# Packed attention and a mixture of experts: the values of both halves multiplied in one burst, a gate chain with fewer VectorE operations, and one addition moved to ScalarE

## The chip, the cores and the metric

The kernel runs on one core of one Trainium2 chip. The metric is the device time in microseconds (us), the median of three runs; less is better. A core has TensorE (PE, matmuls; PEld is its weight load), VectorE (DVE), ScalarE (ACT), GpSimd (POOL) and SyncE (SP, which here only issues DMAs). Each engine works through its own instructions in the order in which they were written, and waits for the others by semaphores.

## The reference, cut to what matters

q, k and v are 8 batches x 8 heads x 576 x 64, p (the "packs") is 8 x 8 x 32 x 64. The attention runs twice: the packs attend over the keys, and the queries attend over the 32 packed rows. Its result feeds a mixture of 8 experts.

```python
def sm_attn(qq, kk, vv):
    s = scale * np.matmul(qq, kk.transpose(0, 1, 3, 2))
    s = s - np.max(s, axis=-1, keepdims=True)
    a = np.exp(s)
    a = a / (np.sum(a, axis=-1, keepdims=True) + 1e-09)
    return np.matmul(a, vv)
p_packed = sm_attn(p, k, v)
out = sm_attn(q, p_packed, p_packed)
...
logits = np.einsum('bsd,de->bse', x, w_gate)          # x: out, 8 x 576 x 512
local_gate = 1.0 / (1.0 + np.exp(-np.einsum('bsd,de->bse', x, w_local).squeeze(-1)))
for b in range(B):
    prev_e = -1
    for s in range(S):
        fresh_e = int(np.argmax(logits[b, s]))
        if s == 0 or local_gate[b, s] < 0.5:
            e = fresh_e
        else:
            e = prev_e if prev_e >= 0 else fresh_e
        prev_e = e
        ls = logits[b, s] - logits[b, s].max()
        p = np.exp(ls)
        p /= p.sum() + 1e-09
        h = np.maximum(x[b, s] @ w1[e], 0.0)          # 512 -> 1024
        out[b, s] = p[e] * (h @ w2[e])                # 1024 -> 512
```

## The kernel before, in words

Each of the 8 batches goes through stages, with its 8 heads in two halves (Q = 0 and 1) of four heads. **Packs:** L496 multiplies packs by keys, L514 takes the scores out of PSUM, L551 transposes the weights of a half (three transposes, then two), L553 copies them to SBUF as `a1T`, and L567 multiplies them by the values: 20 matmuls for a half, each on a tile of 32 columns of the array, which the profile counts as 40 instructions; L583 transposes the result into `ppT`. **Queries:** L614, the softmax over 32 packed rows at L630 to L661 (L652 sums, L654 adds 1e-9, L656 inverts), and the split of the result into a high and a low part (`a2h`, `a2l`). **Gates:** L873 and L881 make the logits, L888 transposes them (`lt`), and a chain of small VectorE operations (L896 to L960) finds the expert's number `e` of the batch (from the first token), the softmax weight `pe`, and a flag `stray` for tokens that would go to another expert. A stray anywhere starts a general branch at the program's end; with these inputs it isn't taken. From `e` the SyncE queue starts the loads of the expert's weights (L987, `w1t`; L994, `w2raw`). L1028 folds the first weights with the packed rows. **Expert:** all of it in pairs of high and low parts. The first layer (L1054) makes six matmuls for half the tokens of 128 hidden units; ScalarE (L1065) and VectorE (L1070, the low part) take the result out and so free its PSUM bank. The second layer (L1094, L1099 and L1103) adds into five accumulators `acc0` to `acc4`. GpSimd forms the low part of the second weights (L1083).

Three PSUM banks are passed around for everything but the accumulators. The order of all engines is fixed when the program is built: each stage is a Python generator, and a planner (`weave`, with the costs of a `Clock`) takes a step of one generator after another, the expert of one batch being the main thread and the attention of the next filling in. A `yield need(...)` is where it may switch; it puts no wait of its own into the program. The expert of a batch takes some 50 us, and in that time the attention and gates of the next one run.

Below, L1054 and so on are lines of the kernel before. In the changed kernel the same lines are 9 to 18 further down: L1063 is the first layer, L1103 and L1108, L1112 the second, L1079 the low part on VectorE, L582 the values, L600 the transposes behind them, L906 and L914 the start of the gate chain, L821 the expert's number.

Of the kernel before, what the change touches and what calls it, by code (L numbers as in the profile page):

```python
# [168 lines left out]
def packed_attn_moe_kernel(  # L169
# [355 lines left out]
    def keys(st, Q):  # L525
# [17 lines left out]
        rooms = ("w2s", "w2s") if st["early"] and Q == 1 else ("a1T", "a1U")  # L543
        yield need(s2, slot=(("w2s", 2),) if st["early"] and Q == 1 else rooms)
# [57 lines left out]
    def queries(st, Q):  # L602
# [262 lines left out]
    def gates(st, expert=None):  # L865
# [31 lines left out]
        mxb = mx.unsqueeze(2).broadcast_to([128, NB, E])  # L897
        v0 = tile_([128, 1], F32, "v0")
# [471 lines left out]
```

## Time and profile before

| what | before |
|---|---|
| median of 3 runs | 428.78 us (428.70 to 429.36) |
| profiled execution: its time, its span | 428.42 us, 426.6 us |
| busy share: TensorE, VectorE, ScalarE, GpSimd | 97%, 63%, 44%, 26% |
| chain that ended last: TensorE, VectorE, ScalarE | 85%, 10%, 2% |

The span is the part of an execution between its first and last recorded instruction. The chain that ended last is followed back from the last instruction, at each step to what released it; its shares say on whom the end waited.

### The profile page before, as it was taken

How to read it: one execution, taken by the hardware profiler on the slowest of the kernel's cores; microseconds unless marked ns; L12 is line 12 of the kernel's file. 1: busy time of each engine (PE TensorE's matmuls, PEld its weight loads, DVE VectorE, ACT ScalarE, POOL GpSimd, SP SyncE). 2: the span in 40 equal slices, each digit the busy share in tenths (PEclk: the TensorE clock that was granted, in tenths of full speed). 3: DMA queues.
4: the chain of work that ended last, by engine and by line, in shares of the span. 5: the costliest groups of instructions: out<-in, count | busy, mean ns of one | idle time of the engine just before them, and what ended most of it. 6: DMA issues, size and time to landing. Idle time of an engine off the chain costs nothing.

```text
span 426.6 us, 9843 instructions
## 1 busy us (share of the span) xinstructions
PE 411.9 (97%) x3735; PEld 317.2 (74%) x3736; DVE 269.0 (63%) x771; ACT 187.5 (44%) x438; POOL 111.1 (26%) x123
## 2 busy tenths in 40 slices
PE   8899999999999999999999998999989999999994
PEld 6676766876777787678768885788857888688882
DVE  4597688685976597667933888348772696422122
ACT  2564434553435443564354541645335443443221
POOL 1005022421541224115312161122511136123220
PEclk9999999999999999999999999999999999999998
DMA  8789749974996593959986947489191212721003
GB/s 225 236 305 231 140 96 324 179 224 104 320 174 212 146 191 77 383 153 167 246 291 110 174 147 258 153 157 224 62 346 28 98 40 87 285 98 37 2 1 115
DMA packets 160909, 72.98 MB, mean 171 GB/s; under 512 B 131170, under 2 KB 139610, under 8 KB 160858
## 3 DMA queue, kind: packets, MB, share of 16 engines
q1 hardware_dynamic: 160858, 72.32, 65.0%
q8 instruction: 30, 0.49, 0.5%
q14 instruction: 21, 0.17, 0.1%
HBM read 62.87 MB, written 9.44 MB: 169 GB/s over the span
## 4 chain that ended last, share of the span: by engine, by line
PE 85%; DVE 10%; ACT 2%; DMA 1%; issue 1%; SPq 0%; DVEq 0%; ACTq 0%
PE acc L1094 40%; PE bank L1054 23%; PE bank L1028 4%; PE acc L1099 3%; PE acc L1103 3%; PE bank L567 2%; PE bank L551 2%; PE bank L614 2%; DVE qn L453 2%; DMA raw<-in_k_dram 1%; PE bank L496 1%; DVE h L1070 1%; PE bank L873 1%; DVE vc L901 1%; DVE df L931 1%
## 5 line engine op out<-in xcount | busy, mean ns | idle before, releaser
L1094 PE MATMUL acc<-w2s,h 128*128 128x512 f32 x768 | 209.7, 404 | 0.0
L1094 PEld LDWEIGHTS acc<-w2s,h 128*128 128x128 f32 x768 | 134.7, 188 | 34.3 <-issue 11.9
L1083 POOL TENSOR_TENSOR w2s<-w2raw,w2s 128x512 fp32r<-128x512 f32 x64 | 85.7, 1341 | 263.7 <-ACT w2s L1081 246.4
L1070 DVE SCALAR_TENSOR_TENSOR h<-bank,h 128x64 fp32r<-128x64 f32 (+3 forms) x192 | 61.5, 347 | 81.6 <-ACT h L1065 80.6
L1065 ACT ACTIVATE h<-bank 128x288 fp32r<-128x288 f32 (+2 forms) x128 | 52.8, 412 | 113.2 <-PE bank L1054 106.0
L1054 PEld LDWEIGHTS bank<-a2h,wph 128*128 128x128 f32 x256 | 45.4, 188 | 24.8 <-issue 6.5
L1054 PE MATMUL bank<-a2h,wph 128*128 128x288 f32 (+2 forms) x256 | 57.8, 307 | 4.7 <-DVE gsm L940 2.9
L1054 PE MATMUL bank<-a2l,wph 128*128 128x288 f32 (+2 forms) x256 | 54.9, 296 | 0.0
L1054 PE MATMUL bank<-a2h,wpl 128*128 128x288 f32 (+2 forms) x256 | 54.8, 295 | 0.0
L1054 PEld LDWEIGHTS bank<-a2h,wpl 128*128 128x128 f32 x256 | 41.2, 188 | 0.0
L1054 PEld LDWEIGHTS bank<-a2l,wph 128*128 128x128 f32 x256 | 40.9, 188 | 0.0
L1081 ACT CAST w2s<-w2raw 128x512 fp32r<-128x512 f32 x64 | 39.5, 617 | 0.2
L1038 DVE TENSOR_TENSOR wpl<-bank,wph 128x512 fp32r<-128x512 f32 (+1 forms) x32 | 20.0, 664 | 18.1 <-ACT wph L1035 18.1
L1035 ACT CAST wph<-bank 128x512 fp32r<-128x512 f32 (+1 forms) x32 | 16.8, 576 | 24.1 <-PE bank L1028 24.1
L1099 PE MATMUL acc<-w2s,h 128*128 128x512 f32 x64 | 26.4, 412 | 0.0
L1103 PE MATMUL acc<-w2s,h 128*64 128x512 f32 x64 | 25.3, 395 | 0.0
L669 POOL TENSOR_TENSOR a2l<-a2t,a2h 128x576 fp32r<-128x576 f32 x14 | 20.0, 1439 | 10.7 <-ACT a2h L667 8.2
L1123 ACT ACTIVATE o<-acc,pe 128x512 f32<-128x512 f32 x23 | 15.8, 688 | 11.3 <-PE acc L1094 11.0
L632 DVE STREAM_TRANSPOSE sT<-bank 128x288 f32<-128x288 f32 x28 | 11.8, 460 | 11.4 <-ACT gate L630 10.9
L599 DVE STREAM_TRANSPOSE qn<-qn 128x1152 f32<-128x1152 f32 x14 | 19.0, 1365 | 0.0
L553 ACT COPY a1T<-bank 116x384 f32<-116x384 f32 (+1 forms) x28 | 11.6, 428 | 12.3 <-PE bank L551 11.9
L453 DVE STREAM_TRANSPOSE qn<-qn 128x1152 f32<-128x1152 f32 x12 | 16.3, 1360 | 0.1
(190 smaller groups left out, 427.8 us busy)
## 6 DMA issues: line engine op xcount, KB each, us to landing
w2raw<-in_moe_w_dram SPq DMA_DIRECT2D x64, 256.0 KB, 7.8
w1t<-in_moe_w_dram SPq DMA_DIRECT2D x15, 1024.0 KB, 5.4
kv<-in_v_dram SPq DMA_DIRECT2D x16, 560.0 KB, 9.8
out_dram<-o SPq DMA_DIRECT2D x32, 256.0 KB, 3.4
qn<-in_q_dram SPq DMA_DIRECT2D x28, 288.0 KB, 4.9
qn<-in_k_dram SPq DMA_DIRECT2D x24, 288.0 KB, 5.2
raw<-in_k_dram SPq DMA_DIRECT2D x4, 576.0 KB
raw<-in_q_dram SPq DMA_DIRECT2D x2, 576.0 KB
```

Source lines behind the costliest of these rows:

```text
L453: nc.vector.transpose(out=kT, in_=kT)
L599: nc.vector.transpose(out=qT, in_=qT)
L669: nc.gpsimd.tensor_tensor(out=a2l, in0=a2t, in1=a2h.bitcast(F32), op=ALU.subtract)
L1038: nc.vector.tensor_tensor(out=lo[:, Q, cols], in0=ts[Q][:, :width], in1=hi[:, Q, cols].bitcast(F32), op=ALU.subtract,)
L1054: nc.tensor.matmul(out=t[:, :width], lhsT=st["wp"][c // 4][wi][:, Q, fs], rhs=a2[ai][Q][:, ts], start=(n == 0), stop=(n == 5),)
L1065: nc.scalar.activation(out=h[:, lo:hi], in_=t[:, :hi - lo], func=AF.Relu)
L1070: nc.vector.scalar_tensor_tensor(out=h[:, dst:dst + z - a], in0=t[:, a:z], scalar=0.0, in1=h[:, lo + a:lo + z].bitcast(F32), op0=ALU.max, ...
L1081: nc.scalar.copy(out=w[:, 0], in_=raw)
L1083: rest.tensor_tensor(out=w[:, 1], in0=raw, in1=w[:, 0].bitcast(F32), op=ALU.subtract)
L1094: nc.tensor.matmul(out=acc, lhsT=hs[hi], rhs=w[:, wi], start=(c == 0 and n == 0), stop=(c == NC - 1 and n == 2),)
L1099: nc.tensor.matmul(out=acc, lhsT=h[:, 512:S + TAIL], rhs=w[:, 0], start=(c == 0), stop=False, skip_group_check=True,)
L1103: nc.tensor.matmul(out=acc[0:TAIL], lhsT=h[:, 512:S], rhs=w[:, 1], start=False, stop=(c == NC - 1), skip_group_check=True,)
```

## The change

Three edits, and what the planner makes of them. First, the values: the generator `keys` of each half ended with its own burst L567; now both halves end in one generator, `packed_keys`, which multiplies both (80 instructions) behind one another into one bank, scales both, transposes both and copies them out once. The first batch, which goes by halves, stays as it was. The buffers of the transposed weights become two pairs, those of the packed rows three for both halves instead of six for one. Second, the gate chain: the subtraction of the maximum (`under`) is made once and serves the expert's code `vc` and the exponent; the softmax weight of the chosen expert is taken by its column in a multiplication on GpSimd, where a mask, a product and a reduction stood; the local gate and the stray flags are worked out once for all batches (`strays`). Per batch the chain has 9 VectorE operations where it had 21. Third, the addition of 1e-9 at L654 goes from VectorE to ScalarE (L672).

```diff
-    "kv": 2, "qn": 3, "p_in": 2, "q_in": 1, "zz": 2, "a1": 2, "a1T": 1, "a1U": 1, "ppT": 6, "sT": 2, "a2t": 2,
+    "kv": 2, "qn": 3, "p_in": 2, "q_in": 1, "zz": 2, "a1": 2, "a1T": 2, "a1U": 2, "ppT": 3, "sT": 2, "a2t": 2,
...
-        rooms = ("w2s", "w2s") if st["early"] and Q == 1 else ("a1T", "a1U")
-        yield need(s2, slot=(("w2s", 2),) if st["early"] and Q == 1 else rooms)
+        rooms = ("a1T", "a1U")
+        yield need(s2, slot=rooms)
...
-        yield need(*a1T, st["v", Q], slot="zz", banks=1)
+        st["turned", Q] = a1T, rs
+        if st["early"]:
+            yield from packed_keys(st, (Q,))
+        elif Q == NQ - 1:
+            yield need(when=lambda: ("turned", 0) in st)
+            yield from packed_keys(st, range(NQ))
+
+    def packed_keys(st, Qs):
+
+        if 0 in Qs:
+            st["ppq"] = tile_([128, NQ, 128], F32, "ppT")
+            clock.edges[st["ppq"].tensor.name] = (128,)
+        a1T, rs = zip(*(st["turned", Q] for Q in Qs))
+        yield need(*(x for y in a1T for x in y), *vs, slot="zz", banks=1)
         pp = bank()
-        for c in range(NV):
-            rows = slice(0, VP if c == 0 else VP - 1)
-            for h in range(HQ):
-                nc.tensor.matmul(
-                    out=pp[32 * h:32 * h + 32, :D],
-                    lhsT=a1T[c // J3][rows, c % J3, 32 * h:32 * h + 32],
-                    rhs=st["v", Q][rows, h, D * c:D * c + D],
-                    start=(c == 0), stop=(c == NV - 1),
-                )
-        give(*a1T, st["v", Q])
-        zz = tile_([128, 2, D], F32, "zz")
-        wide = pp[:, :D].unsqueeze(1).broadcast_to([128, 2, D])
-        if st["early"]:
-            nc.vector.tensor_scalar(out=zz, in0=wide, scalar1=rs, scalar2=None, op0=ALU.mult)
+            for c in range(NV):
+                rows = slice(0, VP if c == 0 else VP - 1)
+                for h in range(HQ):
+                    nc.tensor.matmul(
+                        out=pp[32 * h:32 * h + 32, D * n:D * n + D],
+                        lhsT=a1T[n][c // J3][rows, c % J3, 32 * h:32 * h + 32],
+            wide = pp[:, D * n:D * n + D].unsqueeze(1).broadcast_to([128, 2, D])
+            if st["early"]:
+                nc.vector.tensor_scalar(out=zz[:, n], in0=wide, scalar1=rs[n], scalar2=None, op0=ALU.mult)
+            else:
+                nc.scalar.activation(out=zz[:, n], in_=wide, func=AF.Copy, scale=rs[n][:, 0:1])
         give(pp)
         yield need(zz, banks=1)
         tp = bank()
-        nc.tensor.transpose(out=tp[:, :128], in_=zz.rearrange("a r d -> a (r d)"), identity=ident)
+        for n, Q in enumerate(Qs):
+            nc.tensor.transpose(out=tp[:, 128 * n:128 * n + 128], in_=zz[:, n].rearrange("a r d -> a (r d)"), identity=ident)
         give(zz)
-        ppq = tile_([128, 128], F32, "ppT")
-        nc.scalar.copy(out=ppq, in_=tp[:, :128])
+        lo, hi = Qs[0], Qs[-1] + 1
+        nc.scalar.copy(out=st["ppq"][:, lo:hi], in_=tp[:, :128 * len(Qs)].rearrange("a (q x) -> a q x", x=128))
         give(tp)
-        st["ppT"][Q] = ppq
+        for Q in Qs:
+            st["ppT"][Q] = st["ppq"][:, Q]
...
-        nc.vector.tensor_scalar(out=sm, in0=sm, scalar1=1e-9, scalar2=None, op0=ALU.add)
+        nc.scalar.activation(out=sm, in_=sm, func=AF.Copy, bias=1e-9)
...
+        under = tile_([128, NB, E], F32, "under")
+        yield need(mx)
+        nc.vector.tensor_tensor(out=under, in0=lg, in1=mx.unsqueeze(2).broadcast_to([128, NB, E]), op=ALU.subtract)
             vc = tile_([128, NB, E], F32, "vc")
-            nc.vector.tensor_tensor(out=vc, in0=lg, in1=mxb, op=ALU.is_equal)
-            yield need(vc)
-            nc.vector.tensor_tensor(out=vc, in0=vc, in1=code.unsqueeze(1).broadcast_to([128, NB, E]), op=ALU.mult)
+            yield need(under)
+            nc.vector.scalar_tensor_tensor(
+                out=vc, in0=under, scalar=0.0, in1=code.unsqueeze(1).broadcast_to([128, NB, E]), op0=ALU.is_equal, op1=ALU.mult,
+            )
-
-            yield need(codes_all, st["e0"])
-            e0 = nc.gpsimd.value_load(st["e0"][0:1, 0:1], min_val=0, max_val=E - 1)
-            nc.gpsimd.tensor_copy(out=v0, in_=code[:, bass.ds(e0, 1)])
-            nc.gpsimd.tensor_copy(out=v0_all[:, b:b + 1], in_=v0)
-            yield need(v0)
...
-        nc.vector.tensor_tensor(out=ex, in0=lg, in1=mxb, op=ALU.subtract)
-        sel = tile_([128, E], F32, "sel")
-        nc.vector.tensor_scalar(out=sel, in0=code, scalar1=v0, scalar2=None, op0=ALU.is_equal)
-        yield need(ex)
-        nc.scalar.activation(out=ex, in_=ex, func=AF.Exp)
+        yield need(under)
+        nc.scalar.activation(out=ex, in_=under, func=AF.Exp)
-            gz = tile_([128, NB], F32, "gz")
-            nc.scalar.activation(out=gz, in_=lt[:, :, E], func=AF.Exp, scale=-1.0)
-            df = tile_([128, NB], F32, "df")
-            nc.vector.tensor_scalar(out=df, in0=cd, scalar1=v0, scalar2=None, op0=ALU.not_equal)
+            nc.scalar.activation(out=fresh_all[:, b], in_=lt[:, :, E], func=AF.Exp, scale=-1.0)
-        nc.vector.tensor_tensor(out=ex, in0=ex, in1=sel.unsqueeze(1).broadcast_to([128, NB, E]), op=ALU.mult)
-        if expert is None:
-            yield need(gz)
-            nc.vector.tensor_scalar(out=gz, in0=gz, scalar1=1.0, scalar2=None, op0=ALU.add)
-        if expert is None:
-            yield need(gz)
-            nc.vector.reciprocal(out=gz, in_=gz)
-        yield need(ex)
-        nc.vector.reduce_sum(out=pe, in_=ex, axis=AX.X)
         if expert is None:
-            fr = fresh_all[:, b]
-            yield need(gz)
-            nc.vector.tensor_scalar(out=fr, in0=gz, scalar1=0.5, scalar2=None, op0=ALU.is_lt)
-            nc.vector.memset(fr[0:1, 0:1], 1.0)
-        yield need(sm, pe)
-        nc.vector.tensor_tensor(out=pe, in0=pe, in1=sm, op=ALU.mult)
-        if expert is None:
-            yield need(fresh_all, df)
-            nc.vector.tensor_tensor(out=df, in0=df, in1=fr, op=ALU.mult)
-            yield need(df)
-            nc.vector.reduce_max(out=stray[:, b:b + 1], in_=df, axis=AX.X)
+            yield need(codes_all, st["e0"])
+            expert = nc.gpsimd.value_load(st["e0"][0:1, 0:1], min_val=0, max_val=E - 1)
+            nc.gpsimd.tensor_copy(out=v0_all[:, b:b + 1], in_=code[:, bass.ds(expert, 1)])
             st["done"] = True
+        yield need(sm)
+        nc.gpsimd.tensor_tensor(out=pe, in0=ex[:, :, bass.ds(expert, 1)].squeeze(2), in1=sm, op=ALU.mult)
         st["pe"] = pe
...
+    def strays(st):
+
+        yield need(when=lambda: all("done" in x for x in sts))
+        nc.vector.tensor_scalar(out=fresh_all, in0=fresh_all, scalar1=1.0, scalar2=None, op0=ALU.add)
+        nc.vector.reciprocal(out=fresh_all, in_=fresh_all)
+        nc.vector.tensor_scalar(out=fresh_all, in0=fresh_all, scalar1=0.5, scalar2=None, op0=ALU.is_lt)
+        nc.vector.memset(fresh_all[0:1, :, 0:1], 1.0)
+        df = sb.tile([128, B, NB], F32, name="df", bufs=1)
+        yield need(codes_all, v0_all)
+        nc.vector.tensor_tensor(out=df, in0=codes_all, in1=v0_all.unsqueeze(2).broadcast_to([128, B, NB]), op=ALU.not_equal)
+        nc.vector.tensor_tensor(out=df, in0=df, in1=fresh_all, op=ALU.mult)
+        nc.vector.reduce_max(out=stray, in_=df.rearrange("a b n -> a (b n)"), axis=AX.X)
+        st["strays"] = True
...
+                yield need(stray, banks=1, when=lambda: "strays" in sts[B - 1])
-                nc.tensor.matmul(out=tot[0:1, 0:1], lhsT=red, rhs=ones_col, start=True, stop=True)
+                nc.tensor.matmul(out=tot[0:1, 0:1], lhsT=stray, rhs=ones_col, start=True, stop=True)
```

On VectorE the gate stage of one of the middle batches reads so before (`lt` are the logits, L1070 frees the bank of a first-layer product, `qn` and `p_in` are keys and packs of the batch after):

```order
L888 STREAM_TRANSPOSE lt<-bank_3642 128x160
L1070 SCALAR_TENSOR_TENSOR h<-bank_3634,h 128x224
L1070 SCALAR_TENSOR_TENSOR h<-bank_3634,h 128x64
L896 TENSOR_REDUCE gmx<-lt 128x5
L901 TENSOR_TENSOR vc<-lt,gmx 128x40
L903 TENSOR_TENSOR vc<-vc,code 128x40
L906 TENSOR_REDUCE codes_all<-vc 128x5
L803 TENSOR_SCALAR e_3687<-codes_all 1x1
L453 STREAM_TRANSPOSE qn<-qn 128x4x288
L1070 SCALAR_TENSOR_TENSOR h<-bank_3676,h 128x288
L920 TENSOR_TENSOR ex<-lt,gmx 128x40
L922 TENSOR_SCALAR sel<-code,v_3669 128x8
```

and so with the change, from the same transpose of the logits on:

```order
L906 STREAM_TRANSPOSE lt<-bank_3531 128x160
L914 TENSOR_REDUCE gmx<-lt 128x5
L453 STREAM_TRANSPOSE qn<-qn 128x4x288
L917 TENSOR_TENSOR under<-lt,gmx 128x40
L1079 SCALAR_TENSOR_TENSOR h<-bank_3557,h 128x224
L1079 SCALAR_TENSOR_TENSOR h<-bank_3557,h 128x64
L921 SCALAR_TENSOR_TENSOR vc<-under,code 128x40
L926 TENSOR_REDUCE codes_all<-vc 128x5
L821 TENSOR_SCALAR e_3587<-codes_all 1x1
L939 TENSOR_REDUCE gsm<-ex 128x5
L417 STREAM_TRANSPOSE p_in<-p_in 128x256
L453 STREAM_TRANSPOSE qn<-qn 128x4x288
```

One `qn` transpose, `under` and an L1079 now stand ahead of `vc` and of the expert's number `e`; `sel`, `df` and the second product of `vc` are gone, and the second transpose and the L1079 that ends this piece come sooner after `e`.

On TensorE the values of one of these batches read so before (`kv` are the values, `zz` the scaled result):

```order
L567 MATMUL bank_3917<-kv,a1T 32x64 x20
L1094 MATMUL acc_3533<-w2s,h 128x512 x3
L583 MATMUL bank_3949<-ident,zz 128x128
L1054 MATMUL bank_3953<-a2h,wph 128x288 x2
L1054 MATMUL bank_3953<-a2l,wph 128x288 x2
L1054 MATMUL bank_3953<-a2h,wpl 128x288 x2
L551 MATMUL bank_3962<-ident,a_3802 116x128 x3
L551 MATMUL bank_3968<-ident,a_3802 116x128 x2
L1094 MATMUL acc_3546<-w2s,h 128x512 x3
L1099 MATMUL acc_3554<-w2s,h 128x512
L1103 MATMUL acc_3554<-w2s,h 64x512
L567 MATMUL bank_3982<-kv,a1T 32x64 x20
```

and so with the change:

```order
L1103 MATMUL acc_3422<-w2s,h 128x512 x3
L1103 MATMUL acc_3427<-w2s,h 128x512 x3
L582 MATMUL bank_3816<-kv,a1T 32x64 x40
L1103 MATMUL acc_3432<-w2s,h 128x512 x3
L1063 MATMUL bank_3888<-a2h,wph 128x288 x2
L1063 MATMUL bank_3888<-a2l,wph 128x288 x2
L1063 MATMUL bank_3888<-a2h,wpl 128x288 x2
L600 MATMUL bank_3895<-ident,zz 128x128 x2
L1103 MATMUL acc_3445<-w2s,h 128x512 x3
```

Two bursts with ten rows of other work between them have become one, between two second-layer groups, and the two transposes stand together.

A further place on TensorE, in the fifth batch, is shown with the banks' numbers, since the planner gives banks out anew. Before, the nearest place of its kind reads:

```order
L1028 MATMUL bank1_3280<-w1t_3035,ppT_2818 32x512 x4
L1094 MATMUL acc1_2878<-w2s_3154,h_3153 128x512 x3
L551 MATMUL bank0_3294<-ident_72,a1_3123 116x128 x3
L1094 MATMUL acc2_2882<-w2s_3154,h_3153 128x512 x3
L1054 MATMUL bank0_3304<-a2h_1972,wph_2658 128x288
L1054 MATMUL bank0_3304<-a2h_1973,wph_2658 128x288
```

and with the change:

```order
L1037 MATMUL bank2_3096<-w1t_2964,ppT_2566 32x512 x4
L1037 MATMUL bank0_3097<-w1t_2964,ppT_2566 32x512 x4
L1103 MATMUL acc2_2797<-w2s_2941,h_2940 128x512 x3
L551 MATMUL bank1_3116<-ident_72,a1_2998 116x128 x3
L1063 MATMUL bank1_3125<-a2h_1908,wph_2515 128x288
L1063 MATMUL bank1_3125<-a2h_1909,wph_2515 128x288
L1063 MATMUL bank1_3125<-a2l_1910,wph_2515 128x288
L1063 MATMUL bank1_3125<-a2l_1911,wph_2515 128x288
```

Before, a second-layer group stands between the three transposes into a bank and the next use of that bank; now the first layer follows the transposes into the same bank1 at once. In the second batch the changed order has one more such pair (L551 into bank2, then L1063 into bank2).

## Rows read from the trace of the kernel before

**Rows 1.** Page, part 1: each engine's busy time, share of the span, instructions.
```profile
span 426.6 us, 9843 instructions
...
PE 411.9 (97%) x3735; PEld 317.2 (74%) x3736; DVE 269.0 (63%) x771; ACT 187.5 (44%) x438; POOL 111.1 (26%) x123
```

**Rows 2.** TensorE's waits: tile, line, releaser; total us, times, longest.
```profile
PE bank L1054 <- DVE gsm L940: 2.9, 2, 1.5
```

**Rows 3.** One stretch: PE, PEld, DVE, ACT, POOL busy (instructions), clock, DMA share, GB/s.
```profile
308.00:316.00 8.00, 6.52 (x59) 4.03 (x57) 7.33 (x28) 1.74 (x5) 1.66 (x5) 1.00 0.84 297
```

**Rows 4.** TensorE timeline: start, us, line, operation, tiles, count, [idle, releaser].
```profile
310.60 0.72 PE L496 MATMUL bank<-qn,p_in 64*32 64x288 f32 x16
312.80 0.51 PE L1054 MATMUL bank<-a2h,wph 128*128 128x288 f32 x2 [1.48 <-DVE gsm L940]
...
316.00 1.09 PE L1028 MATMUL bank<-w1t,ppT 64*32 64x512 f32 x16
```

**Rows 5.** VectorE timeline, same stretch.
```profile
304.53 0.35 DVE L888 STREAM_TRANSPOSE lt<-bank 128x160 f32<-128x160 f32 x1 [1.86 <-PE bank L881]
...
305.42 1.14 DVE L901 TENSOR_TENSOR vc<-lt,gmx 128x40 f32<-128x40 f32 x1
306.60 0.20 DVE L903 TENSOR_TENSOR vc<-vc,code 128x40 f32<-128x40 f32 x1
...
307.24 1.38 DVE L453 STREAM_TRANSPOSE qn<-qn 128x1152 f32<-128x1152 f32 x1
308.55 0.42 DVE L1070 SCALAR_TENSOR_TENSOR h<-bank,h 128x288 fp32r<-128x288 f32 x1
308.89 0.18 DVE L920 TENSOR_TENSOR ex<-lt,gmx 128x40 f32<-128x40 f32 x1
...
309.12 0.43 DVE L417 STREAM_TRANSPOSE p_in<-p_in 128x256 f32<-128x256 f32 x1
...
310.74 1.19 DVE L931 TENSOR_SCALAR df<-codes_all,v 128x5 f32<-128x5 f32 x1
...
312.14 0.51 DVE L1070 SCALAR_TENSOR_TENSOR h<-bank,h 128x224 fp32r<-128x224 f32 x2
```

**Rows 6.** GpSimd timeline, same stretch.
```profile
310.60 1.27 POOL L1083 TENSOR_TENSOR w2s<-w2raw,w2s 128x512 fp32r<-128x512 f32 x1 [2.19 <-ACT w2s L1081]
```

**Rows 7.** TensorE timeline around one values burst, 277.2 to 279.6 us.
```profile
277.24 0.39 PE L1099 MATMUL acc<-w2s,h 128*128 128x512 f32 x1
277.47 0.40 PE L1103 MATMUL acc<-w2s,h 128*64 128x512 f32 x1
277.80 0.77 PE L567 MATMUL bank<-kv,a1T 116*32 116x64 f32 x40
278.50 0.53 PE L1054 MATMUL bank<-a2h,wph 128*128 128x288 f32 x2
278.87 0.43 PE L1054 MATMUL bank<-a2l,wph 128*128 128x288 f32 x2
279.13 0.43 PE L1054 MATMUL bank<-a2h,wpl 128*128 128x288 f32 x2
```

**Rows 8.** TensorE timeline, batch 0: two values bursts in a row.
```profile
13.82 1.33 PE L567 MATMUL bank<-kv,a1T 116*32 116x64 f32 x80
15.08 0.33 PE L583 MATMUL acc<-ident,zz 128*128 128x128 f32 x1
```

**Rows 9.** TensorE timeline: the matmul behind three transposes of scores.
```profile
269.16 0.48 PE L1099 MATMUL acc<-w2s,h 128*128 128x512 f32 x1
```

**Rows 10.** ScalarE timeline: the copy that empties those transposes' bank.
```profile
269.44 0.48 ACT L553 COPY a1T<-bank 116x384 f32<-116x384 f32 x1 [0.58 <-PE bank L551]
```

**Rows 11.** One ScalarE line: duration ns min/median/max, first and last start.
```profile
L928 ACT ACTIVATE gz<-lt x8: 196/198/220, 47.8 to 358.3; 128x5 f32<-128x5 f32 x8
```

**Rows 12.** SyncE's queue: the issue of a batch's first-layer weights.
```profile
308.19 1.01 SPq L987 DMA_DIRECT2D w1t<-in_moe_w_dram  x2
```

**Rows 13.** Page, part 6: DMA issues, KB each, median us to landing.
```profile
w1t<-in_moe_w_dram SPq DMA_DIRECT2D x15, 1024.0 KB, 5.4
```

More of the change, by code (lines that the diff above doesn't have):

```diff
@@ L254, in packed_attn_moe_kernel @@
     fresh_all = const.tile([128, B, NB], F32, name="fresh_all")
-    stray = const.tile([128, B], F32, name="stray")
+    stray = const.tile([128, 1], F32, name="stray")
     def at(src, b):
@@ L573, in keys @@
-        give(*a1T, st["v", Q])
-        zz = tile_([128, 2, D], F32, "zz")
-        wide = pp[:, :D].unsqueeze(1).broadcast_to([128, 2, D])
-        if st["early"]:
-            nc.vector.tensor_scalar(out=zz, in0=wide, scalar1=rs, scalar2=None, op0=ALU.mult)
-        else:
-            nc.scalar.activation(out=zz, in_=wide, func=AF.Copy, scale=rs[:, 0:1])
+        st["turned", Q] = a1T, rs
[4 more added lines that the diff above has]
+            yield from packed_keys(st, range(NQ))
@@ new lines, in packed_keys @@
+    def packed_keys(st, Qs):
[3 more added lines that the diff above has]
+        a1T, rs = zip(*(st["turned", Q] for Q in Qs))
+        vs = [st["v", Q] for Q in Qs]
+        yield need(*(x for y in a1T for x in y), *vs, slot="zz", banks=1)
+        pp = bank()
+        for n, Q in enumerate(Qs):
[5 more added lines that the diff above has]
+                        lhsT=a1T[n][c // J3][rows, c % J3, 32 * h:32 * h + 32],
+                        rhs=vs[n][rows, h, D * c:D * c + D],
+                        start=(c == 0), stop=(c == NV - 1),
+                    )
+            give(*a1T[n], vs[n])
+        zz = tile_([128, len(Qs), 2, D], F32, "zz")
+        for n, Q in enumerate(Qs):
+            wide = pp[:, D * n:D * n + D].unsqueeze(1).broadcast_to([128, 2, D])
[3 more added lines that the diff above has]
+                nc.scalar.activation(out=zz[:, n], in_=wide, func=AF.Copy, scale=rs[n][:, 0:1])
@@ L582, in keys @@
         tp = bank()
-        nc.tensor.transpose(out=tp[:, :128], in_=zz.rearrange("a r d -> a (r d)"), identity=ident)
+        for n, Q in enumerate(Qs):
+            nc.tensor.transpose(out=tp[:, 128 * n:128 * n + 128], in_=zz[:, n].rearrange("a r d -> a (r d)"), identity=ident)
         give(zz)
-        ppq = tile_([128, 128], F32, "ppT")
-        nc.scalar.copy(out=ppq, in_=tp[:, :128])
+        lo, hi = Qs[0], Qs[-1] + 1
+        nc.scalar.copy(out=st["ppq"][:, lo:hi], in_=tp[:, :128 * len(Qs)].rearrange("a (q x) -> a q x", x=128))
         give(tp)
-        st["ppT"][Q] = ppq
+        for Q in Qs:
+            st["ppT"][Q] = st["ppq"][:, Q]
     def turn_queries(st, Q):
@@ L896, in gates @@
         nc.vector.reduce_max(out=mx, in_=lg, axis=AX.X)
[L897 to L898 removed]
+        under = tile_([128, NB, E], F32, "under")
+        yield need(mx)
+        nc.vector.tensor_tensor(out=under, in0=lg, in1=mx.unsqueeze(2).broadcast_to([128, NB, E]), op=ALU.subtract)
         if expert is None:
             vc = tile_([128, NB, E], F32, "vc")
[L901 to L903 removed]
+            yield need(under)
+            nc.vector.scalar_tensor_tensor(
+                out=vc, in0=under, scalar=0.0, in1=code.unsqueeze(1).broadcast_to([128, NB, E]), op0=ALU.is_equal, op1=ALU.mult,
+            )
             cd = codes_all[:, b]
@@ L1198, in chunks @@
                 tc.mark_branch_hint_location("general", engines=list(engines_all))
-                yield need(stray, banks=1, when=lambda: all("done" in x for x in sts))
-                red = sb.tile([128, 1], F32, name="red", bufs=1)
-                nc.vector.reduce_max(out=red, in_=stray, axis=AX.X)
+                yield need(stray, banks=1, when=lambda: "strays" in sts[B - 1])
                 tot = bank()
-                nc.tensor.matmul(out=tot[0:1, 0:1], lhsT=red, rhs=ones_col, start=True, stop=True)
+                nc.tensor.matmul(out=tot[0:1, 0:1], lhsT=stray, rhs=ones_col, start=True, stop=True)
                 some = sb.tile([1, 1], I32, name="some", bufs=1)
@@ L1241, in weave @@
                 threads.insert(0, Thread(weights(st), started, True))
+                if started == B - 1:
+                    threads.append(Thread(strays(st), started))
                 started += 1
```

6 lines of the change are left out of this document (5 added, 1 removed).

## Prediction

> **What bounds the kernel now.** I read the page's first part, then the waits, then the stretches of time around the longest waits, then each engine's timeline there. The page shows TensorE busy for 411.9 of 426.6 us; VectorE has 63%, ScalarE 44%, GpSimd 26% [rows 1]. So only two things pay: fewer microseconds of TensorE's own work, and fewer of the 14.7 us in which it stands still. The largest wait in the list is the first layer L1054, twice, 2.9 us together, put down to VectorE's `gsm` L940 [rows 2]. From 308 to 316 us TensorE is busy for only 6.52 of 8 us, and VectorE for 7.33 at a granted clock of 1.00 [rows 3]: there VectorE is the bound. TensorE ends L496 at 311.32 and restarts with L1054 at 312.80, 1.48 us later [rows 4]. The name L940 misleads, since the first layer reads nothing of the gates. What it needs is a PSUM bank, and the L1070 that frees one runs from 312.14 to 312.65 [rows 5], .15 us ahead of the restart. VectorE works without a gap from the logits' transpose at 304.53 to there, 8.12 us for a TensorE that has 6.79 us of work in that time (304.53 to 311.32). Of the 8.12 us, two operations on a few columns are far too long: L901 1.14 where its like, L903, takes .20, and L931 1.19 on 128x5 [rows 5]. The second runs beside GpSimd's L1083, 310.60 to 311.87 [rows 6], and ends right behind it.
>
> **The sum** is made for the profiled execution, 428.42 us (span 426.6 and 1.8 around it); the median of the runs shown is 428.78, .36 more, which I add at the end.
>
> **Values in one burst.** One half's burst takes .70 us (277.80 to 278.50), two alone 1.40; batch 0 runs the same 80 instructions in a row in 1.26 (13.82 to 15.08) [rows 7, 8], .14 less. At the burst's entry, a second-layer matmul takes .33 (277.47 to 277.80) where the one before it takes .23, so .10; behind it the first pair of L1054 takes .37 where the next takes .26, so .11 [rows 7]. A merge drops one entry and one exit: .35 us. Of the seven batches that merge, one (the second) loses less, as its first burst stood right behind L1028, another burst of narrow tiles: .14 there. Together 6 x .35 + .14 = **-2.24 us**. From below: if entry and exit come back at another place, 7 x .14 = -.98. The two transposes together I cost at nothing, as they are the same two. The values' loads now start when the one burst frees both buffers, the first half's later than before; the packs, keys and queries behind them on SyncE's queue come later by as much. The cover is long: bursts are at 278 [rows 7], the next batch's keys are first touched at 307.24 [rows 5].
>
> **Gate chain.** 12 of 21 VectorE operations go from each batch. What decides is the queue from the logits to the L1079 that frees the bank which TensorE next lacks. From the rows of one stage, start to start [rows 5]: logits, two L1070 and maximum .89 (304.53 to 305.42); one key transpose 1.31 (307.24 to 308.55); `under` at most .23 (what `ex` and `sel` took together, 308.89 to 309.12); `vc`, codes and `e` .64 (306.60 to 307.24, now with the one fused operation in place of L903); the sum `gsm` again at most .23; packs and the second key transpose 1.62 (309.12 to 310.74); L1079 .34 (308.55 to 308.89). Sum 5.26, and .15 to the restart. TensorE's work until it needs that bank is by the new order the same but for one pair of half-block matmuls, .46 (two at .23, [rows 7]): 6.79 - .46 = 6.33. So there is .9 us to spare, and both stalls go: **-2.90 us** [rows 2]. A three-operand operation with both inputs in SBUF, as the new `vc`, is not in the trace; its bounds are L903's .20 and, if GpSimd holds it, L901's 1.14 [rows 5]. I take the lower, as GpSimd is busy for 26% only [rows 1]; with one such hold the queue is 6.35, still level with 6.33. The multiplication for `pe` on GpSimd lies between nothing and the 1.27 of a 128x512 one [rows 6]; behind it on that engine stand the L1092 of the next chunks. I cost it at nothing, since GpSimd stands idle for 74% of the span; that idle time is the cover. The strays' seven operations run once, in the last batch, where no gate chain follows, and I cost them at nothing; the cover is the whole last expert, as the flag is read only near the end.
>
> [...]
>
> **1e-9 on ScalarE.** 14 small operations leave VectorE; ScalarE gets 14 of about .20 (as L928, [rows 11]). Queued behind each on ScalarE is an L1074 that takes a first-layer bank out, and TensorE waits for such banks. ScalarE is idle for 56% [rows 1], and that is the cover: 0. Without it 14 x .20 = +2.8 at worst; at best VectorE's relief returns some tenths.
>
> **What the new order adds.** At two places (the second and the fifth batch) the first layer follows three transposes L551 into the very bank that they filled. It must wait until ScalarE's L553 has emptied it. At such a group before, the next matmul, into another bank, starts at 269.16 [rows 9], while the copy ends at 269.92 [rows 10]: .76 us, and .15 for the restart as above, .91. Twice: **+1.82 us**. It is less only if ScalarE gets to it earlier than there, more (by a relu, some .4) if the copy finds ScalarE taken. Before, a second-layer group stood between and covered it.
>
> **Sum:** 428.42 - 2.24 - 2.90 + 1.82 = 425.10 for a profiled execution, and with .36 a median of **425.5 us**. The smaller waits I leave as they are.
>
> **Rivals.**
> *B, the new waits cost nothing*, because the first layer arrives late there for other reasons, or TensorE catches up in a later wait that then is shorter: 425.5 - 1.8 = 423.7. For it: 14.7 us of standing still are spread over many short waits. Against: TensorE's stages around there are full before, and nothing covers a wait of .9 that has no work behind it.
> *A, GpSimd holds `under` and `vc` both*: VectorE's queue grows by 2 x .94 to 7.14, and with .15 it is .96 beyond TensorE's 6.33. In the three middle batches whose gates stand in this order that is 2.9 us: 425.5 + 2.9 = 428.4, no change. For it: of one chain before, two operations were held [rows 5]. Against: two holds in each of three chains need GpSimd to be running at both moments.
> *C, slower: the first weights come late.* `e` is now .36 later at best, as a key transpose stands ahead of it (.89 + 1.31 + .23 + .64 = 3.07 after the logits; before 2.71). Before, the weights were issued at 308.19 [rows 12] and landed some 5.4 us later [rows 13], 9.1 after the logits, for an L1028 at 316.00 [rows 4], which is 10.0 after them without the stall. Now they land at 9.4 for about the same 10.0, with five transposes more ahead of it: .6 us or a bit more to spare. If `e` is held by both collisions (1.9) and SyncE's queue, behind the output stores that now stand just ahead, adds .5, L1037 waits 1.8 us in each of three batches: 425.5 + 5.4 = 431. It decides the sign once `e` is some 2 us later than worked out, in all three.
> *The change doesn't do what it says*: nothing speaks for it, as the order shows the merged bursts and shorter chains; what could be is that a merged burst saves only .14, which the bound above holds.
>
> **Chances and range.** The forecast has .61, B .15, A .14, C .10. About what a measurement can tell from no change is .2%, .86 us: faster is below 427.9, slower above 429.6. Faster: .61 of the forecast but .01, B's .15, and a third of A (fewer holds) .05, so .80. Same: .01 and A's other .09, .10. Slower: C, .10. The likeliest case by itself spans 424.4 (values' sum in full, waits at .76 and less) to 426.8 (merges at .98). The range for all reaches to B below and to A above: 423.1 to 428.2; C and the outer ends of A and B, 2 in 10, are left out.
>
> **What would show it.** In the changed profile: seven bursts of 80 values instructions at some 1.26 us each, with one slow entry and exit; no wait of L1063 over 1 us with VectorE's gates as releaser; `vc` at .2 us; two waits of .7 to .9 us of L1063 on ScalarE's L553, in the second and fifth batch. It is wrong if L1037 waits for a DMA, if `under` or `vc` last about 1.1 us beside an L1092 in several batches, or if L1063 waits for the bank behind an L672 on ScalarE.

## The result, and the profile after

The changed kernel takes 422.09 us (median of 6 runs, 421.74 to 423.18), the one before 428.97 on the same chip: ratio 0.9842, 95% interval 0.9830 to 0.9854, so 6.9 us less. The forecast was 425.5 us, its range 423.1 to 428.2: the sign was right, the gain was twice as large as forecast, and the time lies 1.0 us below the range.

The page of the changed kernel, part 1 and the shares of the chain that ended last:

```profile
span 420.4 us, 9792 instructions
...
PE 408.7 (97%) x3735; PEld 319.6 (76%) x3736; DVE 252.4 (60%) x667; ACT 188.7 (45%) x445; POOL 112.6 (27%) x123
...
PE 91%; DVE 3%; ACT 2%; DMA 1%; issue 1%; DVEq 0%; ACTq 0%
```

Of the 6.2 us that the span lost [rows 1], 3.2 are TensorE's busy time, the rest is time in which it stood still. VectorE's share of the chain fell from 10% to 3%. The largest waits of TensorE now (line, releaser: total us, times, longest):

```profile
PE acc L224 <- DVE warm L217: 1.3, 1, 1.3
PE bank L1063 <- ACT a1T L553: 1.2, 2, 0.6
PE acc L551 <- ACT a L534: 0.8, 1, 0.8
PE bank L1063 <- DVE a L514: 0.7, 1, 0.7
```

The two waits on the gates [rows 2] are gone, and the two that the new order was to add are there. The gate stage that answers to [rows 3] (same columns) is full:

```profile
300.00:308.00 8.00, 8.00 (x69) 5.75 (x68) 6.25 (x20) 2.80 (x8) 2.12 (x6) 1.00 0.40 138
```

VectorE's timeline there, beside [rows 5]:

```profile
299.34 0.35 DVE L906 STREAM_TRANSPOSE lt<-bank 128x160 f32<-128x160 f32 x1 [1.11 <-PE bank L899]
...
299.90 1.38 DVE L453 STREAM_TRANSPOSE qn<-qn 128x1152 f32<-128x1152 f32 x1
301.20 0.16 DVE L917 TENSOR_TENSOR under<-lt,gmx 128x40 f32<-128x40 f32 x1
301.43 0.52 DVE L1079 SCALAR_TENSOR_TENSOR h<-bank,h 128x224 fp32r<-128x224 f32 x2
301.87 0.19 DVE L921 SCALAR_TENSOR_TENSOR vc<-under,code 128x40 f32<-128x40 f32 x1
...
302.32 0.14 DVE L821 TENSOR_SCALAR e<-codes_all 1x1 int32<-1x1 f32 x1
...
304.13 0.42 DVE L1079 SCALAR_TENSOR_TENSOR h<-bank,h 128x288 fp32r<-128x288 f32 x1
```

From the logits to the L1079 that frees the next bank it takes 4.79 us (299.34 to 304.13), and with the .34 that the prediction counted for that L1079 5.13, where it had 5.26. TensorE's timeline goes from L496 into L1063 without a gap, as against [rows 4]:

```profile
304.90 0.72 PE L496 MATMUL bank<-qn,p_in 64*32 64x288 f32 x16
305.54 0.54 PE L1063 MATMUL bank<-a2h,wph 128*128 128x288 f32 x2
```

The new fused `vc`, and `under`, over all eight batches (duration ns min/median/max):

```profile
L921 DVE SCALAR_TENSOR_TENSOR vc<-under,code x8: 189/199/201, 44.5 to 348.7; 128x40 f32<-128x40 f32 x8
```

```profile
L917 DVE TENSOR_TENSOR under<-lt,gmx x8: 156/190/726, 44.3 to 348.1; 128x40 f32<-128x40 f32 x8
```

`vc` was never held, 201 ns at most; `under` was in two batches (726 and 549 ns, each ending .05 to .06 us behind a GpSimd instruction that ran beside it), so never both in one chain. In the kernel before, L901 and L931 took 1.13 to 1.19 us five times, the two of [rows 5] among them, and each of the five ended some .06 us behind an L1083 that ran beside it; beside that L901 it is this one:

```profile
305.22 1.29 POOL L1083 TENSOR_TENSOR w2s<-w2raw,w2s 128x512 fp32r<-128x512 f32 x1
```

In three batches `vc` started shortly ahead of a GpSimd instruction that reads and writes SBUF; in the stage above that is this one:

```profile
302.05 1.29 POOL L1092 TENSOR_TENSOR w2s<-w2raw,w2s 128x512 fp32r<-128x512 f32 x1 [1.61 <-ACT w2s L1090]
```

The merged burst takes the 1.26 us of [rows 8], here (319.11 to 320.37) and in the six other batches that merge:

```profile
319.11 1.33 PE L582 MATMUL bank<-kv,a1T 116*32 116x64 f32 x80
320.37 0.98 PE L1103 MATMUL acc<-w2s,h 128*128 128x512 f32 x3
```

And the first of the two new waits, on TensorE and on ScalarE:

```profile
47.59 0.49 PE L551 MATMUL bank<-ident,a 128*116 128x128 f32 x3
48.70 0.56 PE L1063 MATMUL bank<-a2h,wph 128*128 128x320 f32 x2 [0.62 <-ACT a1T L553]
```

```profile
47.11 1.07 ACT L1044 CAST wph<-bank 128x512 fp32r<-128x512 f32 x2 [0.52 <-PE bank L1037]
48.17 0.48 ACT L553 COPY a1T<-bank 116x384 f32<-116x384 f32 x1
```

The copy ends at 48.65 and L1063 starts .05 later: the hop is shorter than the .15 of the sum.

All this is as forecast or a little better. What the sum had no term for shows in the costliest group of all, the 768 matmuls of the second layer, before and after (busy us, mean ns of one | idle before):

```profile
L1094 PE MATMUL acc<-w2s,h 128*128 128x512 f32 x768 | 209.7, 404 | 0.0
```

```profile
L1103 PE MATMUL acc<-w2s,h 128*128 128x512 f32 x768 | 205.5, 399 | 0.0
```

Nothing in the code of these matmuls has changed, and yet they take 4.2 us less. Part of it is fewer slow starts behind bursts of other lines: of the 768, 61 took over 470 ns before and 50 do now, each the first behind such a burst (none behind the first layer), where the others take 396 and 392 on average. For the rest I took, from the traces, the time from start to start of second-layer matmuls in an unbroken row (some 460 to 530 pairs in each trace): 233.2 ns on average before, 230.4 after. Below this is called the spacing. It moves by up to .5 ns with the choice of pairs, so less than that is not read from it. Times 768 the difference is 2.2 us.

### The profile page after: what moved, and what is told of

Same layout as the page of the kernel before. It is cut to its first block, busy times and chain, and to the rows that moved or that the text cites. A ratio compares the mean times of both kernels' runs of the same rounds, so it can differ in the third digit from the quotient of the medians.

```text
span 420.4 us, 9792 instructions
## 1 busy us (share of the span) xinstructions
PE 408.7 (97%) x3735; PEld 319.6 (76%) x3736; DVE 252.4 (60%) x667; ACT 188.7 (45%) x445; POOL 112.6 (27%) x123
## 4 chain that ended last, share of the span: by engine, by line
PE 91%; DVE 3%; ACT 2%; DMA 1%; issue 1%; DVEq 0%; ACTq 0%
PE acc L1103 43%; PE bank L1063 24%; PE bank L1037 4%; PE acc L1108 4%; PE acc L1112 3%; PE bank L582 2%; PE bank L632 2%; PE bank L496 2%; PE bank L551 2%; PE acc L224 1%; DMA w1t<-in_moe_w_dram 1%; PE bank L891 1%; PE acc L432 1%; PE bank L432 1%; DVE sT L723 0%
## 5 line engine op out<-in xcount | busy, mean ns | idle before, releaser
L1103 PE MATMUL acc<-w2s,h 128*128 128x512 f32 x768 | 205.5, 399 | 0.0
L1103 PEld LDWEIGHTS acc<-w2s,h 128*128 128x128 f32 x768 | 135.2, 188 | 31.1 <-issue 9.9
L1092 POOL TENSOR_TENSOR w2s<-w2raw,w2s 128x512 fp32r<-128x512 f32 x64 | 87.7, 1371 | 237.4 <-ACT w2s L1090 235.5
L1079 DVE SCALAR_TENSOR_TENSOR h<-bank,h 128x64 fp32r<-128x64 f32 (+3 forms) x192 | 61.5, 348 | 85.4 <-ACT h L1074 84.4
L1063 PEld LDWEIGHTS bank<-a2h,wph 128*128 128x128 f32 x256 | 45.8, 188 | 20.1 <-issue 5.2
L1063 PE MATMUL bank<-a2h,wph 128*128 128x288 f32 (+2 forms) x256 | 57.8, 307 | 2.2 <-ACT a1T L553 1.2
L1063 PE MATMUL bank<-a2l,wph 128*128 128x288 f32 (+2 forms) x256 | 55.1, 296 | 0.0
L1063 PE MATMUL bank<-a2h,wpl 128*128 128x288 f32 (+2 forms) x256 | 54.8, 295 | 0.0
L1063 PEld LDWEIGHTS bank<-a2h,wpl 128*128 128x128 f32 x256 | 41.3, 188 | 0.0
L1063 PEld LDWEIGHTS bank<-a2l,wph 128*128 128x128 f32 x256 | 41.2, 189 | 0.0
L1108 PE MATMUL acc<-w2s,h 128*128 128x512 f32 x64 | 26.3, 411 | 0.0
L617 DVE STREAM_TRANSPOSE qn<-qn 128x1152 f32<-128x1152 f32 x14 | 19.1, 1366 | 0.0
L1108 PEld LDWEIGHTS acc<-w2s,h 128*128 128x128 f32 x64 | 12.0, 188 | 8.4 <-issue 6.0
```

What stands on the lines that cost most here:

```text
L617: nc.vector.transpose(out=qT, in_=qT)
L1063: nc.tensor.matmul(out=t[:, :width], lhsT=st["wp"][c // 4][wi][:, Q, fs], rhs=a2[ai][Q][:, ts], start=(n == 0), stop=(n == 5),)
L1079: nc.vector.scalar_tensor_tensor(out=h[:, dst:dst + z - a], in0=t[:, a:z], scalar=0.0, in1=h[:, lo + a:lo + z].bitcast(F32), op0=ALU.max, ...
L1092: rest.tensor_tensor(out=w[:, 1], in0=raw, in1=w[:, 0].bitcast(F32), op=ALU.subtract)
L1103: nc.tensor.matmul(out=acc, lhsT=hs[hi], rhs=w[:, wi], start=(c == 0 and n == 0), stop=(c == NC - 1 and n == 2),)
L1108: nc.tensor.matmul(out=acc, lhsT=h[:, 512:S + TAIL], rhs=w[:, 0], start=(c == 0), stop=False, skip_group_check=True,)
```

## The experiments

Times are medians; the kernel before took 428.6 to 428.9 us beside them.

**Where the second layer's operands lie (eight runs, every instruction in the same order as in the kernel they start from).** In the kernel before, batch 0 borrowed two `w2s` buffers for its transposed weights, so that the build laid `w2s` ahead of `h` in SBUF; the changed one doesn't (`rooms`), and `w2s` lies right behind `h`. `w2s` is the second layer's moving operand, `h` its weights. First, this alone in the kernel before (run e1; buffers of their own, `a1X`, in place of the borrowed ones):

```diff
-    "kv": 2, "qn": 3, "p_in": 2, "q_in": 1, "zz": 2, "a1": 2, "a1T": 1, "a1U": 1, "ppT": 6, "sT": 2, "a2t": 2,
+    "kv": 2, "qn": 3, "p_in": 2, "q_in": 1, "zz": 2, "a1": 2, "a1T": 1, "a1U": 1, "a1X": 2, "ppT": 6, "sT": 2, "a2t": 2,
...
-        rooms = ("w2s", "w2s") if st["early"] and Q == 1 else ("a1T", "a1U")
-        yield need(s2, slot=(("w2s", 2),) if st["early"] and Q == 1 else rooms)
+        rooms = ("a1X", "a1X") if st["early"] and Q == 1 else ("a1T", "a1U")
+        yield need(s2, slot=(("a1X", 2),) if st["early"] and Q == 1 else rooms)
```

> The kernel before, every instruction in the same order; only the second weights' buffers (w2s) and with them h lie at other SBUF addresses: w2s behind h, as in the changed kernel. Theory 1 (addresses): the steady start-to-start time of second-layer matmuls, 233.3 ns before and 230.3 ns after the change, is set by where these operands lie; then it falls to about 230 here and the time by 2 to 3 us, to about 426. Theory 2 (neighbours): it fell because VectorE and its neighbours do less; then 233 ns and 429.0 us, within 0.4, as before.

426.65 us, ratio 0.9956 (0.9943 to 0.9969); spacing 230.4. Then back again in the changed kernel (e2), by reserving the four `w2s` buffers in batch 0's `keys`:

```diff
-        st["turned", Q] = a1T, rs
+        st["turned", Q] = a1T, rs; [sb.tile([128, 2, DM], F32R, name="w2s", tag="w2s", bufs=4) for _ in range(4 if st["early"] and Q == 0 else 0)]
```

> The changed kernel, every instruction in the same order; w2s ahead of h in SBUF again, near its old address. Theory 1 (addresses): second-layer spacing back to about 233 ns and the time up by 2 to 3 us, to about 425. Theory 2 (neighbours): 230 ns and 422.1 us as it is.

423.88 us, ratio 0.9886 (0.9872 to 0.9900); spacing 233.2. The same group of matmuls in these two, first the kernel before with the new place, then the changed kernel with the old one:

```profile
L1094 PE MATMUL acc<-w2s,h 128*128 128x512 f32 x768 | 207.3, 400 | 0.0
```

```profile
L1103 PE MATMUL acc<-w2s,h 128*128 128x512 f32 x768 | 208.0, 402 | 0.0
```

Both ways the place is worth 1.8 to 2.0 us, and 2.4 to 2.5 of the group's 4.2 us of busy time: shown. The other 1.7 to 1.8 of the 4.2 come without it (209.7 to 208.0, and 207.3 to 205.5); the slow starts are part of that, and I have not taken it apart. Which property of the place counts was asked with six runs, e7 to e12 in this order; each puts a small unused tile (`pad`, here of 32 bytes) ahead of `w2s` or `h` (`...` stands for arguments left out):

```diff
-tiles[c] = (..., tile_([128, 2 * S], F32R, "h"), tile_([128, 2, DM], F32R, "w2s"), set())
+tiles[c] = (..., tile_([128, 2 * S], F32R, "h"), (sb.tile([128, 8], F32, name="pad", ...), tile_([128, 2, DM], F32R, "w2s"))[1], set())
```

> The changed kernel, every instruction in the same order; the second weights' buffers 32 bytes further on in SBUF, behind h as they were, so that they begin at a multiple of 64 bytes like before the change. If the spacing of second-layer matmuls hangs on the start's remainder by 64 bytes, it rises from 230 to about 233 ns and the time by about 2 us, to 424. If it hangs on the region of SBUF (w2s behind h): 230 ns and 422.1 us.

> As the run with w2s ahead of h in SBUF (423.9 us), every instruction in the same order, but w2s 32 bytes further on, so that it begins 32 bytes behind a multiple of 64. If the spacing hangs on that remainder, it falls to about 230 ns and the time to 422.1 us; if on the region, it stays at 233 ns and 423.9 us.

> The changed kernel, every instruction in the same order, w2s ahead of h in SBUF as in the run of 423.9 us, but h 224 bytes further on, so that the distance from h to w2s is a multiple of 512 bytes, as it is in the changed kernel. In the six traces so far the spacing of second-layer matmuls is 230.4 ns where the distance is such a multiple and 232.8 to 233.2 where its remainder by 512 is 288, 320 or 480, on whichever side w2s lies. If that remainder decides: 230.4 ns and 422.1 us. If not (region of SBUF, or w2s's own start): 233 ns and 423.9.

> The changed kernel, every instruction in the same order, w2s 64 bytes further on (remainder of the distance to h by 512 is 64). If only a remainder of zero by 512 is fast: 233 ns, 424 us. If a remainder by 64 decides: 230.4 ns, 422.1 us. A value under 230 would be a better place than the changed kernel's.

> The same with 128 bytes. If a remainder by 128 decides: 230.4 ns and 422.1 us; if only zero by 512 is fast: 233 ns, 424 us.

> The same with 256 bytes. If a remainder by 256 decides: 230.4 ns and 422.1 us; if only zero by 512 is fast: 233 ns, 424 us.

The distance is the address of `h` less that of `w2s`, in bytes, taken from the addresses of the build; its remainder is the same for all four pairs of buffers (the text of e10 counts it the other way round: its 64 is 192 here):

| kernel | w2s | remainder by 64 of w2s's start | remainder by 256 of the distance | spacing, ns | us |
|---|---|---|---|---|---|
| before; e2 | ahead | 0 | 32 | 233.2; 233.2 | 428.97; 423.88 |
| e8 | ahead | 32 | 64 | 232.8 | 423.34 |
| e9 | ahead | 0 | 0 | 230.9 | 422.88 |
| e1; changed | behind | 32 | 0 | 230.4; 230.4 | 426.65; 422.09 |
| e12 | behind | 32 | 0 | 230.5 | 421.92 |
| e7 | behind | 0 | 224 | 232.8 | 424.16 |
| e10 | behind | 32 | 192 | 229.4 | 421.94 |
| e11 | behind | 32 | 128 | 232.1 | 423.42 |

Not the side (e7, e9), not `w2s`'s own start (e8, e9), and not a remainder by 64 (e8, e11): what goes with the spacing in all of them is the remainder by 256 of the distance. Zero and 192 are the good ones of the six that I saw; e12, with 256 in place of 0 by 512, shows that 512 isn't needed. Why it is so is not shown, and a pad also moves the gates' small tiles, which lie behind it; no run moved those alone. Times at like spacing differ by up to .8 us (e7 and e8), so the time follows the spacing only within that. e9's time is .8 us above the changed kernel's, which its interval (0.9841 to 0.9874) does not tell from nothing; its trace has a wait of 1.0 us near the start on a load of the first weights. e10 and e12 are as fast as the changed kernel within the intervals (ratios 0.9840, 0.9823 to 0.9856, and 0.9835, 0.9819 to 0.9852), so no version here clearly beats it. In the runs below, whatever order the planner makes, the spacing stays with the kernel that they start from: 233 to 234 ns in e6, e13, e14 and e16, 230 to 231 in e3, e4, e5 and e15.

**One burst or two.** The changed kernel with a burst for each half (e3):

```diff
         if st["early"]:
             yield from packed_keys(st, (Q,))
-        elif Q == NQ - 1:
-            yield need(when=lambda: ("turned", 0) in st)
-            yield from packed_keys(st, range(NQ))
+        else:
+            yield need(when=lambda: Q == 0 or "ppq" in st)
+            yield from packed_keys(st, (Q,))
```

> The changed kernel with one values burst for each half again (the planner orders them anew). By the sum's term (.35 us for each of six merges, .14 for the seventh) it takes 2.2 us more, about 424.3 us. Rival: entry and exit of a burst come back elsewhere, so that a merge is worth only .14 us: 1.0 more, 423.1. A second rival: the merge costs more than it saves through the longer time that the bank and the values' buffers are held: not slower than 422.1.

423.99 us, ratio 0.9892 (0.9878 to 0.9907): 1.9 us more. In its trace the two same-bank waits (1.2 us) are gone too, while another has come that the changed kernel hasn't:

```profile
PE bank L1063 <- DVE h L1079: 0.7, 1, 0.7
```

So the merged burst itself is probably worth somewhat more than 1.9 here, about 2.4 by these waits, and the new waits take a part back; with the order made anew this is argued and not shown. Then the merge alone in the kernel before (e13: `packed_keys` and its buffers, and a pad that keeps the second layer's distance; the rest as it was):

> The kernel before with the values of both halves in one burst (and its buffers), and nothing else; w2s lies so that its distance to h has the remainder that it had before (32 by 256), so that the second layer's spacing stays at 233 ns. By the sum's term -2.24 us: 426.6, if the planner adds no waits; with one or two new same-bank waits up to 428.4. Rival: merging is worth only 1 us: 427.8.

433.77 us, ratio 1.0110 (1.0092 to 1.0129): 5.1 us slower, a miss for all that I had written. Its waits and its windows (columns as in [rows 2, 3]; L1072 is the first layer there, L891 the gates' first matmul):

```profile
PE bank L1072 <- DVE gsm L958: 4.3, 3, 1.4
PE bank L891 <- DVE a2t L679: 1.7, 1, 1.7
```

```profile
78.00:84.00 6.00, 3.71 (x44) 2.47 (x43) 4.42 (x13) 1.63 (x3) 2.57 (x5) 0.83 1.24 196
84.00:90.00 6.00, 6.00 (x22) 4.99 (x21) 4.98 (x18) 2.42 (x6) 1.05 (x1) 0.60 0.99 160
```

With the long gate chain still there, three stages now wait on it where two did, and at 78 to 84 us, in the second batch, TensorE stood still for 2.3 of 6 us, its waits put down to the queries' results (`a2t`, `a2l`). Its granted clock was 0.83 there and 0.60 over the next 6 us. In this one execution that costs up to (.17 + .40) x 6 = 3.4 us of full-speed work, a bound estimated from these two clocks. The five executions say less: with mean granted clocks of .998, .995, .992, .989 and .989 they took 432.85, 433.77, 432.43, 434.34 and 434.47 us, so about 2 us at most go with the clock, and some 4 of the 5.1 are there without it. With the orders that this planner makes, the merge pays with the shorter chain and loses with the long one.

**The gate chain.** The changed kernel with `gates` of before and no `strays` (e4):

> The changed kernel with the gate chain of before (21 VectorE operations for each batch, strays found for each batch). If the chain's length made the two stalls, they come back: first-layer waits on VectorE of some 1.4 us each, 2.9 us in all, about 425 us. Rival: the stalls went because the planner ordered the stage anew after the merge: no such waits, 422 to 422.5 us.

429.73 us, ratio 1.0024 (1.0011 to 1.0038): 7.6 us more, not 3. Of the two stalls on the gates only one came back. Here too TensorE stood still in the second batch, and the granted clock from 80 to 86 us was 0.72:

```profile
PE bank L891 <- DVE a2t L679: 1.4, 1, 1.4
PE bank L1072 <- DVE gsm L958: 1.1, 1, 1.1
PE bank L1072 <- POOL a2l L687: 1.0, 1, 1.0
```

```profile
80.00:86.00 6.00, 4.88 (x37) 3.99 (x38) 4.96 (x20) 2.51 (x6) 2.96 (x4) 0.72 1.14 180
```

With smaller ones, its list has some 5 us of waits that the changed kernel hasn't. The clock is in the median too: the three executions with a mean granted clock of .997 and more took 428.4 to 428.6 us, the seven with .988 to .995 took 429.7 to 430.8. So without the lower clock the old chain costs the changed kernel about 6.4 us. The kernel before with the new `gates` and `strays` alone (e6):

> The kernel before with the new gate chain and the strays found once, and nothing else; operands at the same SBUF addresses as before. By the sum's term the two waits of the first layer on the gates' VectorE work go, 2.9 us: 425.7 to 426.0 us, second-layer spacing still 233 ns. Rival: a shorter chain lets the planner order the stage anew, so that more (or other) waits go or come: outside 425 to 427.

425.80 us, ratio 0.9935 (0.9922 to 0.9949): 3.1 us less, as forecast. The gate stage is full, though one operation of this chain took 1.15 us:

```profile
308.00:316.00 8.00, 8.00 (x78) 4.73 (x77) 5.35 (x20) 2.51 (x6) 1.44 (x2) 1.00 0.92 332
```

```profile
304.67 1.15 DVE L899 TENSOR_TENSOR under<-lt,gmx 128x40 f32<-128x40 f32 x1
```

The planner ordered e6 anew too, so the run shows what the edit brings with its order, and not the shorter chain by itself.

**The addition of 1e-9.** Undone in the changed kernel (e5, the edit shown), then made alone in the kernel before (e14, the same edit the other way round); the planner orders both anew:

```diff
-        nc.scalar.activation(out=sm, in_=sm, func=AF.Copy, bias=1e-9)
+        nc.vector.tensor_scalar(out=sm, in0=sm, scalar1=1e-9, scalar2=None, op0=ALU.add)
```

> The changed kernel with the addition of 1e-9 in the queries' softmax on VectorE again. By the sum's term the move is worth nothing: 422.1 us, within 0.4. Rival: VectorE's relief (14 operations of .13 to .84 us) is worth some tenths: 422.5 to 423.5. Second rival: the hop over ScalarE costs more than it saves: under 421.7.

> The kernel before with the addition of 1e-9 on ScalarE and nothing else (the planner orders anew; addresses as before). If the addition is worth the 1.5 us that undoing it cost in the changed kernel: 427.3 us. If that was the planner's other order there: 428.8 plus or minus what the new order brings.

423.63 us (0.9881, 0.9865 to 0.9897), 1.5 more; and 426.09 us (0.9941, 0.9926 to 0.9956), 2.6 less. Then both with the order held (e15 and e16), by telling the planner the cost of the other engine's operation (`as_if` is a new field of the `Clock`; shown for the changed kernel):

```diff
-        self.rate = 300.0
+        self.rate, self.as_if = 300.0, None
...
-        kind = str(inst.engine).split(".")[-1]
+        kind = str(inst.engine).split(".")[-1] if not self.as_if else self.as_if
...
-        nc.scalar.activation(out=sm, in_=sm, func=AF.Copy, bias=1e-9)
+        clock.as_if = "Activation"; nc.vector.tensor_scalar(out=sm, in0=sm, scalar1=1e-9, scalar2=None, op0=ALU.add); clock.as_if = None
```

> The changed kernel with the addition of 1e-9 on VectorE and every other instruction in the order of the changed kernel (the planner is told the cost of the ScalarE operation). If VectorE's relief is worth the 1.5 us: 423.6. If it was the order that the planner made of it: 422.1, within 0.3.

> The kernel before with the addition on ScalarE and every other instruction in the order of before. If VectorE's relief pays by itself: 427.3 to 428.3. If not: 428.8, within 0.3, or a little more for the hop over ScalarE.

422.52 us (0.9856, 0.9841 to 0.9871), .4 more; and 428.19 us (0.9986, 0.9977 to 0.9995), .5 less. The .4 is within the intervals of the two (0.9830 to 0.9854 for the changed kernel), the .5 is just clear of none. So VectorE's relief itself is worth about half a microsecond in the kernel before and at most about that in the changed one, and most of the 1.5 and 2.6 is the planner's other order. In e14 the two gate waits don't stand in the list any more; its largest on a bank is the first row here. In e16, with the order held, they stay, .7 us shorter (second row):

```profile
PE bank L1054 <- DVE h L1070: 0.9, 2, 0.7
```

```profile
PE bank L1054 <- DVE gsm L940: 2.2, 2, 1.1
```

How e14, with all 21 operations, loses the stalls can be read from VectorE's timeline in the same stage:

```profile
302.03 0.35 DVE L888 STREAM_TRANSPOSE lt<-bank 128x160 f32<-128x160 f32 x1 [1.18 <-PE bank L881]
302.64 0.44 DVE L901 TENSOR_TENSOR vc<-lt,gmx 128x40 f32<-128x40 f32 x1
...
305.47 0.72 DVE L920 TENSOR_TENSOR ex<-lt,gmx 128x40 f32<-128x40 f32 x1
...
307.87 0.41 DVE L1070 SCALAR_TENSOR_TENSOR h<-bank,h 128x288 fp32r<-128x288 f32 x1
308.21 0.21 DVE L931 TENSOR_SCALAR df<-codes_all,v 128x5 f32<-128x5 f32 x1
```

The L1070 that frees the bank which TensorE next lacks stands ahead of L931 here, and the two longest gate operations ahead of it took .44 and .72, where L901 and L931 took 1.14 and 1.19 [rows 5]. From the logits to the end of that L1070 it is 6.25 us (302.03 to 308.28), where it was 8.12.

## Why the prediction was wrong, by its own steps

- **What bounds the kernel:** right. TensorE's work, and VectorE's queue in the gate stages; where the queue is shorter the waits go (e6, e14).
- **Gate chain, -2.90:** right, -3.1 by itself (e6), and the queue came to 5.13 where 5.26 was worked out. But it isn't this edit's alone: e14 removes the same two waits by another order and with shorter gate operations ahead (.44 and .72). In the stage of [rows 5] the two held operations are 1.9 us longer than their like, more than the stall of 1.48, so part of the term may be holds that did not come; the sum had no price for that, and no run tells the two apart. The gains of the edits don't add up (-3.1, -2.6 and, for the merge alone, +5.1, against -6.9 for all with the new places).
- **Values, -2.24:** right in size with the short chain (e3: 1.9 us; 1.26 for each of the seven bursts), wrong as a term that stands by itself: alone it costs 5.1 (e13).
- **1e-9 on ScalarE, 0:** wrong. It was worth 1.5 us in the changed kernel (e5): at most some half of a microsecond by VectorE's relief (e15, not clear of nothing) and the rest by the order. I had costed the operation, not the order that a planner makes when its costs change.
- **New waits, +1.82:** the two are there, 1.2 us together in place of 1.82: the hop was .05, not .15, and the copy came sooner: at the first of them it ended .57 after TensorE was free (48.08 to 48.65), not .76. So rival B was not it, though its time, 423.7, lies nearer the result than the forecast's.
- **The sum:** it had no term for the place of the buffers. The diff changes the buffers' counts and batch 0's `rooms`, and with them the distance of the second layer's operands: 1.8 to 2.0 us (e1, e2). This is the step that failed: a term put at nothing without a word. The changed kernel with its operands at the old distance takes 423.9 us (e2), inside the range. With 1.5 for the addition and .6 for the new waits that comes to 4.0 for a gap of 3.4 us. The place was measured with the order held; the 1.5 was not, and it overlaps with the others, so this is a tally and not a proof.
- **Rivals:** A didn't come (`vc` and `under` were never both held), C neither (L1037 waited once on its weights, .4 us). In three batches, the one above among them, `vc` started ahead of an L1092 (301.87 and 302.05) and took .19, and in the other five no long GpSimd instruction ran beside it; so this trace doesn't show the fused form held, nor that it can't be.

## What to carry to other kernels

When a diff changes the number or the first use of buffers, compare the addresses of the operands of the costliest matmuls before and after, and measure the start-to-start time of that group: 1% of the time of 768 matmuls was over half of the error here. Where a planner orders the program, a changed cost can be a changed order: price it by holding the order once, as `as_if` does. And the edits that relieve the same queue were neither additive nor independent here; the merge, which loads it, lost 5.1 us alone (e13) and won 1.9 with the short chain (e3).

## What the runs showed of the hardware that I had not expected

The spacing of 128x512 matmuls hung on where weights and moving operand lie to one another: 229.4 to 233.2 ns, with the instruction order unchanged. And a stage in which TensorE stood still for 2.3 of 6 us was followed by 6 us at a granted clock of 0.60 (e13); in e4 the clock was 1.00 from 74 to 80 us, where TensorE stood still for 1.3 us, and 0.72 from 80 to 86, where it did so for 1.1, and the executions with the lower mean clock took 1.1 to 2.4 us longer.
